# One half row of w2 loaded into 32 partitions by a transfer with an outer dimension of four

## The chip, the core and the metric

The kernel runs on one core of a Trainium2 chip. The metric is the time of one execution on the device in microseconds (us); the median of three runs of the kernel before is 138.66 us (138.64 to 138.8). Weights and caches lie in HBM (the chip's main memory). Transfers (DMAs) bring them to SBUF, the on-chip memory of 128 partitions; TensorE (PE) multiplies and writes its sums to PSUM; VectorE (DVE), ScalarE (ACT) and GpSimd (POOL) work on SBUF and PSUM; SyncE (SP) issues almost all of the transfers. A transfer is cut into packets, which are carried by 16 DMA engines; the profile's DMA row is the mean busy share of these 16.

## What is computed

One decoding step of a transformer block for four sequences (`x` is 4 x 1 x 1024), in bf16: attention over the last 2048 places of a key and value cache, then a gated feed-forward part.

```python
x = A_x
h = x + _A_ref(_layernorm(x), A_k_cache, A_v_cache, A_wq, A_wo)
# _B_ref(n) with n = _layernorm(h): B, D, F = 4, 1024, 3584
gate = einsum("bsd,df->bsf", n, w1)
up   = einsum("bsd,df->bsf", n, w3)
out  = einsum("bsf,fd->bsd", silu(gate) * up, w2)
h2 = h + out
```

With four sequences every weight is used once, so the kernel is above all a stream of 55.6 MB from HBM.

## The kernel before, in words

One function does everything. The order of the work on each engine is written out by hand (`manual_schedule`); the engines wait for each other by semaphores alone. All streamed data goes through one SBUF tile `ring` (128 partitions, five units of 16384 bf16 values each), whose regions are used again and again: a load must wait until the matmuls that read the old content are done. `load` (L123) issues on SP's queue, in the order wq (two pieces), four k blocks, four v blocks, wo, w1, w3, and then w2.

w2 has F = 3584 rows, viewed as `w2_v[p, fc, n]` with row p*28 + fc: each of the 128 partitions holds 28 of w2's rows, and "row fc" below is the slice of 128 x 1024 values with one fc. `W2B = [13, 8, 4, 2, 1]` (L114) cuts the 28 slices into five groups. The first 13 are loaded right behind w3; the others are issued after the gate matmuls (L507 to L512), the last slice in two halves of 512 columns. So w2 arrives in six transfers, each with its own semaphore, and each shorter than the one before it.

The feed-forward part runs so: gate matmuls (L494) on w1, silu on ACT and DVE (L513 to L516), up matmuls (also L494) on w3, the product `hg` and its transpose `hg_T` (L520, L521 with the helper's line L218). `hg_T[:, fc, :]` is the left operand for slice fc: 128 partitions x 32 columns. Then w2 is used in two styles:

- slices 0 to 20, the groups of 13 and 8: two matmuls of 512 columns each (L538), summed in the PSUM tile `early_ps`. DVE adds the result to `h1`, which holds the residual h (L549);
- slices 21 to 27, the groups of 4, 2 and 1: six matmuls each (L554), four of 128 columns and two of 256, summed in three PSUM tiles `y2_ps`. A matmul with a unit matrix (L565) adds part of `h1`, after the group of four.

At the end ACT copies and DVE adds into `res` (L577, L578, L582), and SP and ACT issue two small output transfers each (L587).

Early in the kernel `x` is loaded by ACT's queue (L135) into 16 partitions of `x_nat`, with a source view whose outer dimension is four, `x_flat.rearrange("b (c n) -> c b n", c=C)`, C = 4. POOL builds constants, a unit matrix `ident` among them (L144 to L183).

Of the kernel before, what the change touches and what calls it, by code (L numbers as in the profile page):

```python
# [10 lines left out]
P = 128  # L11
# [3 lines left out]
BF16 = mybir.dt.bfloat16  # L15
# [6 lines left out]
def kernel(  # L22
# [20 lines left out]
    nc = tc.nc  # L43

    B, _, D = A_x.shape
# [7 lines left out]
    FC = F // P  # L53
    NK = W // P
    C = 4
    R = 32
    S = R // B
    DQ = D // C
# [23 lines left out]
    w2_v = B_w2.rearrange("(p fc) n -> p fc n", fc=FC)  # L82

    const = ctx.enter_context(tc.tile_pool(name="const", bufs=1))
    act = ctx.enter_context(tc.tile_pool(name="act", bufs=1))
# [10 lines left out]
    ring = stream.tile([P, 5 * UNIT], BF16)  # L96

    def at(unit, *shape):
        o = unit * UNIT
        view = ring[:, o : o + int(np.prod(shape))]  # L100
        if len(shape) == 1:
            return view
        names = "abc"[: len(shape)]
        return view.rearrange(
            f"p ({' '.join(names)}) -> p {' '.join(names)}", **dict(zip(names, shape))
        )
# [4 lines left out]
    wo_s = at(3, T, D)  # L111
    w1_s = at(1, KC, F)
    w3_s = at(3, KC, F)
    W2B = [13, 8, 4, 2, 1]  # L114
    w2_s = []
    o = 0
    for i, n in enumerate(W2B):
        if i == 1:
            o = UNIT
        w2_s.append(ring[:, o : o + n * D].rearrange("p (a n) -> p a n", a=n))  # L120
        o += n * D

    def load(dst, src):  # L123
        nc.sync.dma_start(out=dst, in_=src)  # L124
# [13 lines left out]
    for b in range(B):  # L138
# [4 lines left out]
    ident = const.tile([P, P], BF16)  # L143
# [2 lines left out]
    nc.gpsimd.memset(mean_f[:], 1.0 / D)  # L146
    eps_t = const.tile([P, 1], FP32)
    nc.gpsimd.memset(eps_t[:], eps)
    ident_f = const.tile([P, P], FP32)
    nc.gpsimd.tensor_copy(out=ident_f[:], in_=ident[:])  # L150

# [6 lines left out]
        out=same[:], in_=t32[:].rearrange("p (o h) -> p o h", o=1).to_broadcast([P, C, R])  # L158
    )
    gmask = const.tile([P, 1, Hkv], BF16)  # L160
    with nc.allow_low_precision("sums of zeros and a single one"):
        nc.vector.tensor_reduce(
            out=gmask[:, 0], in_=t32[:].rearrange("p (g r) -> p g r", g=Hkv), axis=AX.X, op=ALU.add
# [3 lines left out]
    for j in range(JM):  # L167
# [3 lines left out]
        out=nscale[:], in_=ident_f[:2, :2], scalar=-qscale, op=ALU.mult  # L171
# [5 lines left out]
        out=place[:, : R * C].rearrange("p (h e) -> p h e", e=C)[:, :, C - 1], in_=t32[:]  # L177
# [6 lines left out]
        out=gather[:, :, :B], in_=ident[:].rearrange("p (c b s) -> p c b s", c=C, b=B)[:, :, :, 0]  # L184
# [31 lines left out]
    def transpose_quads(dst, src, n):  # L216

        nc.vector.transpose(  # L218
            out=dst.rearrange("p j r -> p (j r)"), in_=src.rearrange("p (q j) -> p j q", j=n)
        )  # L220
# [8 lines left out]
    for kc in range(KC):  # L229
        for hf in range(2):  # L230
            for c in range(C):
                o = (2 * c + hf) * HALF * Dh
                nc.tensor.matmul(  # L233
                    q_ps[R * c : R * c + R, hf],
                    lhsT=xn_T[:, kc, :],
                    rhs=wq_s[:, kc, o : o + HALF * Dh],
                    start=(kc == 0),
                    stop=(kc == KC - 1),
                    tile_position=(0, R * c),
# [5 lines left out]
    for r in range(REP):  # L245
# [8 lines left out]
        out=Qm[:].rearrange("p b (g y) -> p b g y", y=QW)[:, :, :, :REP],  # L254
        in_=qT_ps[:, :, :, :B].rearrange("p r g b -> p b g r"),
# [154 lines left out]
    small = ps.tile([P, 2, 512], FP32, tag="ktB")  # L410
# [29 lines left out]
    for e in range(C):  # L440
        nc.tensor.matmul(
            on_ps[:],
            lhsT=place[:, C - 1 - e : C - 1 - e + P],
            rhs=om[:, :, e * T : (e + 1) * T],
            start=(e == 0),
            stop=(e == C - 1),
# [6 lines left out]
    for i in range(2):  # L453
        for k in range(2):
            c = i + 2 * k
            nc.tensor.matmul(
                y_ps[R * i : R * i + R, k],
                lhsT=gather[:, c, :],
                rhs=x_nat[:],
                start=(k == 0),  # L460
                stop=False,
                tile_position=(0, R * i),
                skip_group_check=True,
            )
    for t in range(T):
        row = wo_s[:, t].rearrange("p (k i n) -> p i k n", k=2, i=2)
        for i in range(2):
            nc.tensor.matmul(  # L468
                y_ps[R * i : R * i + R],
                lhsT=oP[:, t, :],  # L470
                rhs=row[:, i],
                start=False,
                stop=(t == T - 1),
                tile_position=(0, R * i),
                skip_group_check=True,
            )
    load(w3_s, w3_v)
    load(w2_s[0], w2_v[:, : W2B[0], :])
    h1 = act.tile([P, DQ], FP32)
# [9 lines left out]
    def up_projection(w, out_ps):  # L489
        cols = w.rearrange("p k (c q h j) -> p k c h q j", c=C, h=2, j=FJ)  # L490
        for hf in range(2):
            for kc in range(KC):
                for c in range(C):
                    nc.tensor.matmul(  # L494
                        out_ps[hf][R * c : R * c + R, :],
                        lhsT=hn_T[:, kc, :],
                        rhs=cols[:, kc, c, hf],
                        start=(kc == 0),
                        stop=(kc == KC - 1),
                        tile_position=(0, R * c),  # L500
                    )
# [3 lines left out]
    eg = act.tile([P, 2, FH], FP32, tag="eg")  # L505
    hg = act.tile([P, 2, FH], BF16, tag="hg")
    up_projection(w1_s, [gate_ps[:, hf, :FH] for hf in range(2)])  # L507
    fc = W2B[0]
    for w, n in zip(w2_s[1:], W2B[1:]):
        for h in (slice(0, D),) if n > 1 else (slice(0, D // 2), slice(D // 2, D)):  # L510
            load(w[:, :, h], w2_v[:, fc : fc + n, h])
        fc += n  # L512
    nc.scalar.activation(out=eg[:], in_=gate_ps[:, :, :FH], func=ACT.Exp, scale=-1.0)  # L513
    nc.scalar.activation(out=eg[:], in_=eg[:], func=ACT.Identity, bias=1.0)  # L514
    nc.vector.reciprocal(out=eg[:], in_=eg[:])  # L515
# [2 lines left out]
    hg_T = act.tile([P, FC, R], BF16)  # L518
    for hf in range(2):
        nc.vector.tensor_tensor(out=hg[:, hf], in0=up_ps[hf][:], in1=eg[:, hf], op=ALU.mult)  # L520
        transpose_quads(hg_T[:, FJ * hf : FJ * hf + FJ, :], hg[:, hf], FJ)  # L521


    early_ps = ps.tile([2 * R, 2, DQ], FP32, tag="ktA", name="early_ps")
    DH = DQ // 2
    y2_ps = [
        ps.tile(shape, FP32, tag=tag, name="y2_ps")
        for shape, tag in (([P, DH], "scA"), ([P, DH], "ktB"), ([P, DQ], "scB"))
    ]
    NE = 2  # L530
    FE = sum(W2B[:NE])

    fc = 0
    for w, n in zip(w2_s[:NE], W2B[:NE]):
        for ff in range(n):
            row = w[:, ff].rearrange("p (k i n) -> p i k n", k=2, i=2)
            for i in range(2):
                nc.tensor.matmul(  # L538
                    early_ps[R * i : R * i + R],
                    lhsT=hg_T[:, fc, :],  # L540
                    rhs=row[:, i],
                    start=(fc == 0),
                    stop=(fc == FE - 1),
                    tile_position=(0, R * i),
                )
            fc += 1
    for k in range(2):
        part = h1[2 * R * k : 2 * R * k + 2 * R, :]
        nc.vector.tensor_tensor(out=part, in0=early_ps[:, k], in1=part, op=ALU.add)  # L549
    for m, (w, n) in enumerate(zip(w2_s[NE:], W2B[NE:])):  # L550
        for ff in range(n):
            for t, c, size in ((0, 0, DH), (0, 1, DH), (1, 0, DH), (1, 1, DH), (2, 2, DQ), (2, 3, DQ)):
                o = c * DQ + t % 2 * DH
                nc.tensor.matmul(  # L554
                    y2_ps[t][R * c : R * c + R, :],
                    lhsT=hg_T[:, fc, :],
                    rhs=w[:, ff, o : o + size],
                    start=(fc == FE),
                    stop=(fc == FC - 1),
                    tile_position=(0, R * c),  # L560
                    skip_group_check=True,
                )
            fc += 1
        if m == 0:
            nc.tensor.matmul(  # L565
                y2_ps[1][: 2 * R, :],
                lhsT=ident_f[:, : 2 * R],
                rhs=h1[:, DH:],
                start=False,
                stop=False,  # L570
                skip_group_check=True,
            )
    res = act.tile([P, DQ], BF16)
    for k in range(2):
        part = slice(2 * R * k, 2 * R * k + 2 * R)
        if k == 0:
            nc.scalar.copy(out=res[part, DH:], in_=y2_ps[1][part, :])  # L577
            nc.vector.tensor_tensor(  # L578
                out=res[part, :DH], in0=y2_ps[0][part, :], in1=h1[part, :DH], op=ALU.add
            )  # L580
        else:
            nc.vector.tensor_tensor(  # L582
                out=res[part, :], in0=y2_ps[2][part, :], in1=h1[part, :], op=ALU.add
            )
        for i, eng in enumerate((nc.sync, nc.scalar)):
            c = 2 * k + i
            eng.dma_start(  # L587
                out=out_flat[:, c * DQ : (c + 1) * DQ], in_=res[R * c : R * c + B, :]
# [31 lines left out]
```

## Time and profile before

| what | value |
|---|---|
| median of three runs | 138.66 us |
| the profiled execution: its own time | 138.7 us |
| its span, from first to last instruction | 136.7 us |
| PE, DVE, ACT, POOL busy share of the span | 55%, 37%, 21%, 11% |
| DMA queue of SP: share of 16 engines' span, bytes | 95.3%, 55.58 MB |
| mean rate from HBM over the span | 407 GB/s |
| granted TensorE clock, mean | 0.912 |

The span is 2.0 us shorter than the execution's own time: what lies before the first and behind the last instruction. The engines' shares say little here, since the DMA engines are busy nearly all the time. The page has further parts: the span in 40 slices, the DMA queues, the chain of waits that ended last, the costliest groups of instructions, and the DMA issues. Besides, a trace can be asked for a timeline, for the busy times in chosen stretches, and it keeps each DMA packet (its queue, size, start and duration) and each landing mark, the moment at which one DMA engine reports on a transfer's semaphore that its share is in place. The packets do not say which of the 16 engines carried them.

### The profile page before, as it was taken

How to read it: one execution, taken by the hardware profiler on the slowest of the kernel's cores; microseconds unless marked ns; L12 is line 12 of the kernel's file. 1: busy time of each engine (PE TensorE's matmuls, PEld its weight loads, DVE VectorE, ACT ScalarE, POOL GpSimd, SP SyncE). 2: the span in 40 equal slices, each digit the busy share in tenths (PEclk: the TensorE clock that was granted, in tenths of full speed). 3: DMA queues.
4: the chain of work that ended last, by engine and by line, in shares of the span. 5: the costliest groups of instructions: out<-in, count | busy, mean ns of one | idle time of the engine just before them, and what ended most of it. 6: DMA issues, size and time to landing. Idle time of an engine off the chain costs nothing.

```text
span 136.7 us, 1762 instructions
## 1 busy us (share of the span) xinstructions
PE 74.8 (55%) x762; PEld 40.6 (30%) x762; DVE 49.9 (37%) x50; ACT 28.8 (21%) x32; POOL 15.3 (11%) x41
## 2 busy tenths in 40 slices
PE   0000044959999986029966875994184000946471
PEld 0000011439957852014423323341042000413240
DVE  0000110006526363989799920004100594090022
ACT  3000130025968495104000000000405400000000
POOL 7300060000000000000176333000200000000000
PEclk9999999999999999955999999599959955599999
DMA  4999697999999999998978979969799798999960
GB/s 163 497 454 538 269 537 307 432 417 451 408 432 436 412 436 408 436 585 360 556 326 364 556 326 475 520 285 537 336 470 508 302 520 372 384 423 432 384 245 2
DMA packets 2795, 55.70 MB, mean 408 GB/s; under 512 B 324, under 2 KB 612, under 8 KB 740
## 3 DMA queue, kind: packets, MB, share of 16 engines
q1 hardware_dynamic: 2752, 55.58, 95.3%
q8 instruction: 6, 0.10, 0.3%
q10 hardware_dynamic: 36, 0.01, 0.0%
q14 instruction: 1, 0.01, 0.0%
HBM read 55.58 MB, written 0.01 MB: 407 GB/s over the span
## 4 chain that ended last, share of the span: by engine, by line
DMA 59%; PE 28%; DVE 6%; ACT 3%; SPq 1%; issue 1%; DVEq 0%
DMA ring<-in_B_w_dram 43%; DMA ring<-in_A_wq_dram 15%; PE kt_ps L267 9%; PE sc_ps L290 5%; PE q_ps L233 4%; PE o_ps L381 4%; PE gate L494 3%; DVE P L344 2%; DVE PT L366 2%; ACT ring L271 1%; PE small L381 1%; DVE ring L269 1%; SPq L124 1%; DVE rmax L302 1%; ACT q_sb L243 1%
## 5 line engine op out<-in xcount | busy, mean ns | idle before, releaser
L271 ACT COPY ring<-kt_ps 128x2048 bf16<-128x2048 bf16 x8 | 14.6, 1866 | 7.1 <-PE kt_ps L267 7.1
L267 PE MATMUL kt_ps<-ident,ring 128*128 128x128 bf16 x256 | 15.0, 219 | 0.6 <-DVE Qm L253 0.5
L267 PEld LDWEIGHTS <-ring 128*128 128x128 bf16 x256 | 14.4, 98 | 2.6 <-issue 2.6
L269 DVE COPY ring<-kt_ps 128x2048 bf16<-128x2048 bf16 x8 | 9.8, 1225 | 9.3 <-PE kt_ps L267 9.3
L398 POOL TENSOR_TENSOR o<-od 128x256 f32<-128x256 f32 x4 | 6.8, 1695 | 54.2 <-DVE od L389 54.2
L193 PE MATMUL sums_ps<-both,mean_f 128*128 128x64 f32 x4 | 1.1, 366 | 18.9 <-ACT both L191 18.9
L494 PE MATMUL up<-ring,n_T 128*32 128x448 bf16 x64 | 4.7, 467 | 12.2 <-DMA ring<-in_B_w_dram 12.2
L494 PEld LDWEIGHTS <-n_T 128*32 128x32 bf16 x128 | 4.2, 121 | 20.2 <-DMA ring<-in_B_w_dram 12.7
L344 DVE TENSOR_TENSOR P<-p,gmask 128x2048 bf16<-128x2048 bf16 x4 | 9.1, 2278 | 0.8 <-ACT p L331 0.8
L381 PEld LDWEIGHTS <-PT 128*128 128x128 bf16 x64 | 6.7, 107 | 9.0 <-issue 1.9
L366 DVE STREAM_TRANSPOSE PT<-P 128x2048 bf16<-128x2048 bf16 x4 | 9.2, 2306 | 0.1
L515 DVE RECIPROCAL eg<-eg 128x896 f32<-128x896 f32 x1 | 5.8, 5753 | 9.5 <-ACT eg L514 9.5
L468 PE MATMUL y_ps<-ring,oP 128*32 128x512 bf16 x64 | 8.8, 442 | 0.1
L233 PE MATMUL q_ps<-ring,n_T 128*32 128x512 bf16 x64 | 6.6, 587 | 3.8 <-DMA ring<-in_A_wq_dram 2.0
L381 PE MATMUL o_ps<-ring,PT 128*128 128x512 bf16 x32 | 8.6, 430 | 0.0
L290 PE MATMUL sc_ps<-ring,Qm 128*32 128x512 bf16 x64 | 7.6, 604 | 0.4 <-DVE ring L269 0.4
L538 PE MATMUL early_ps<-ring,hg_T 128*32 128x512 bf16 x42 | 4.9, 379 | 5.1 <-DMA ring<-in_B_w_dram 5.1
L381 PE MATMUL small<-ring,PT 128*128 128x512 bf16 x32 | 7.2, 379 | 0.7 <-DVE rinv L362 0.7
L193 PEld LDWEIGHTS sums_ps<-both,mean_f 128*128 128x128 f32 x4 | 0.8, 248 | 19.4 <-issue 16.9
L494 PE MATMUL gate<-ring,n_T 128*32 128x448 bf16 x64 | 4.6, 458 | 3.2 <-DMA ring<-in_B_w_dram 3.2
L577 ACT CAST res<-y_ps 64x128 bf16<-64x128 f32 x1 | 0.3, 259 | 26.3 <-PE y_ps L554 26.3
L218 DVE STREAM_TRANSPOSE x_T<-x_nat 128x256 bf16<-128x256 bf16 x1 | 0.6, 626 | 13.0 <-DMA x_nat<-in_A_x_dram 13.0
(81 smaller groups left out, 62.5 us busy)
## 6 DMA issues: line engine op xcount, KB each, us to landing
ring<-in_B_w_dram SPq DMA_DIRECT2D x2, 7168.0 KB
ring<-in_A_k_cache_dram SPq DMA_DIRECT2D x4, 2048.0 KB, 25.6
ring<-in_A_v_cache_dram SPq DMA_DIRECT2D x4, 2048.0 KB, 42.9
ring<-in_A_wq_dram SPq DMA_DIRECT2D x1, 7168.0 KB, 21.2
ring<-in_B_w_dram SPq DMA_DIRECT2D x1, 3328.0 KB
ring<-in_B_w_dram SPq DMA_DIRECT2D x1, 2048.0 KB
ring<-in_A_wq_dram SPq DMA_DIRECT2D x1, 1024.0 KB, 4.6
ring<-in_B_w_dram SPq DMA_DIRECT2D x1, 1024.0 KB, 28.1
```

Source lines behind the costliest of these rows:

```text
L233: nc.tensor.matmul(q_ps[R * c : R * c + R, hf], lhsT=xn_T[:, kc, :], rhs=wq_s[:, kc, o : o + HALF * Dh], start=(kc == 0), stop=(kc == KC - 1),
L267: nc.tensor.transpose(out=kt_ps[:, jj], in_=blocks[:, jj, :], identity=ident[:])
L269: nc.vector.tensor_copy(out=blocks, in_=kt_ps[:])
L271: nc.scalar.copy(out=blocks, in_=kt_ps[:])
L290: nc.tensor.matmul(sc_ps[b // 2][R * q : R * q + R, b % 2], lhsT=Qm[:, b, g * R : (g + 1) * R], rhs=kT[:, b, g, q], start=(g == 0), stop=( ...
L344: nc.vector.tensor_tensor(out=P4[:], in0=stage.pop(("p1", b))[:].rearrange("p (x o) -> p x o", o=1).to_broadcast([P, JR * L5, Hkv]), in1=g ...
L366: nc.vector.transpose(out=PT[:].rearrange("p j h -> p (j h)"), in_=stage.pop(("P4", b))[:].rearrange("p x g -> p (x g)"),)
L381: nc.tensor.matmul(o_ps, lhsT=PT[:, i * JM : (i + 1) * JM, :].rearrange("p j h -> p (j h)"), rhs=v_s[b][:, i * JM : (i + 1) * JM, :], star ...
L398: nc.gpsimd.tensor_tensor(out=o2[:], in0=od[:, :2], in1=od[:, 2:], op=ALU.add)
L468: nc.tensor.matmul(y_ps[R * i : R * i + R], lhsT=oP[:, t, :], rhs=row[:, i], start=False, stop=(t == T - 1), tile_position=(0, R * i), ski ...
L494: nc.tensor.matmul(out_ps[hf][R * c : R * c + R, :], lhsT=hn_T[:, kc, :], rhs=cols[:, kc, c, hf], start=(kc == 0), stop=(kc == KC - 1), ti ...
L515: nc.vector.reciprocal(out=eg[:], in_=eg[:])
```

## The change

The second half of w2's last slice is loaded as before. The first half, 128 rows of 512 values (1 KB each), goes into partitions 0 to 31 of `ring`, four rows in each: the view `w2_a` is 32 x 4 x 512. Its source is written with an outer dimension of four, an inner one of 32, and 512 values, and it is the first w2 transfer issued after the gate matmuls instead of the last but one. The groups become `[13, 8, 5, 1, 1]`. The rows then lie in another order in the partitions, so the left operands are brought into this order too: POOL builds `order`, four permuted pieces of the unit matrix; four small matmuls of `order` with the last slice of `hg_T` write `last_ps`, and ACT copies them to `last_T` (32 partitions x 4 x 32). The first half is then multiplied in four steps of 32 partitions, each step four matmuls of 128 columns (`FIRST`), right behind the early groups. The unit-matrix matmul stands before the group of five and reads 64 partitions of `h1` instead of 128. The two matmuls of 256 columns for the second half (`SECOND`) stand last.

```diff
-    W2B = [13, 8, 4, 2, 1]
+    W2B = [13, 8, 5, 1, 1]
...
+    T4 = P // R
+    w2_a = ring[:R, o : o + T4 * D // 2].rearrange("p (t n) -> p t n", t=T4)
...
+    order = const.tile([P, T4, C, R // C], BF16)
+    nc.gpsimd.tensor_copy(
+        out=order[:], in_=ident[:].rearrange("p (q t a) -> p t a q", t=T4, a=C)
+    )
...
     up_projection(w1_s, [gate_ps[:, hf, :FH] for hf in range(2)])
+    HALVES = (slice(0, D // 2), slice(D // 2, D))
+    load(w2_a, w2_v[:, FC - 1, HALVES[0]].rearrange("(y a) n -> a y n", a=C))
     fc = W2B[0]
-    for w, n in zip(w2_s[1:], W2B[1:]):
-        for h in (slice(0, D),) if n > 1 else (slice(0, D // 2), slice(D // 2, D)):
-            load(w[:, :, h], w2_v[:, fc : fc + n, h])
+    for w, n in zip(w2_s[1:-1], W2B[1:-1]):
+        load(w, w2_v[:, fc : fc + n, :])
         fc += n
+    load(w2_s[-1][:, 0, HALVES[1]], w2_v[:, FC - 1, HALVES[1]])
...
+    last_ps = small[:R, 1, : T4 * R].rearrange("p (t r) -> p t r", t=T4)
+    for t in range(T4):
+        nc.tensor.matmul(
+            last_ps[:, t],
+            lhsT=order[:, t].rearrange("p a q -> p (a q)"),
+            rhs=hg_T[:, FC - 1, :],
+            start=True,
+            stop=True,
+        )
+    last_T = act.tile([R, T4, R], BF16)
+    nc.scalar.copy(out=last_T[:], in_=last_ps)
...
+    early(0, 0)
+    early(1, W2B[0])
+    for t in range(T4):
+        late(w2_a[:, t], last_T[:, t], FIRST, start=(t == 0))
     for k in range(2):
         part = h1[2 * R * k : 2 * R * k + 2 * R, :]
         nc.vector.tensor_tensor(out=part, in0=early_ps[:, k], in1=part, op=ALU.add)
...
+    nc.tensor.matmul(
+        y2_ps[1][: 2 * R, :],
+        lhsT=ident_f[: 2 * R, : 2 * R],
+        rhs=h1[: 2 * R, DH:],
...
+    for fc in range(FE, FC - 1):
+        m, ff = (NE, fc - FE) if fc < FE + W2B[NE] else (NE + 1, 0)
+        row = w2_s[m][:, ff]
+        late(row, hg_T[:, fc, :], FIRST, stop=(fc == FC - 2))
+        late(row, hg_T[:, fc, :], SECOND, start=(fc == FE))
+    late(w2_s[-1][:, 0], hg_T[:, FC - 1, :], SECOND, stop=True)
```

`early` and `late` are the old loops as functions: `early` issues the 512-column matmuls of a group, `late` those that the tuple of cuts names.

More of the change, by code (lines that the diff above doesn't have):

```diff
@@ L531, with early, late @@
     FE = sum(W2B[:NE])
[L533 to L537, printed above, removed]
-                nc.tensor.matmul(
[L539 to L544, printed above, removed]
-                )
-            fc += 1
+    def early(i, fc):
+        for ff in range(W2B[i]):
+            row = w2_s[i][:, ff].rearrange("p (k i n) -> p i k n", k=2, i=2)
+            for i2 in range(2):
+                nc.tensor.matmul(
+                    early_ps[R * i2 : R * i2 + R],
+                    lhsT=hg_T[:, fc + ff, :],
+                    rhs=row[:, i2],
+                    start=(fc + ff == 0),
+                    stop=(fc + ff == FE - 1),
+                    tile_position=(0, R * i2),
+                )
+    FIRST = ((0, 0, 0), (0, 1, 0), (1, 0, DH), (1, 1, DH))
+    SECOND = ((2, 2, 0), (2, 3, 0))
+    def late(row, hT, cuts, start=False, stop=False):
+        for t, c, o in cuts:
+            out_ps = y2_ps[t][R * c : R * c + R, :]
+            nc.tensor.matmul(
+                out_ps,
+                lhsT=hT,
+                rhs=row[:, c * DQ + o : c * DQ + o + out_ps.shape[-1]],
+                start=start,
+                stop=stop,
+                tile_position=(0, R * c),
+                skip_group_check=True,
+            )
+    early(0, 0)
+    early(1, W2B[0])
+    for t in range(T4):
+        late(w2_a[:, t], last_T[:, t], FIRST, start=(t == 0))
     for k in range(2):
@@ L549 @@
         nc.vector.tensor_tensor(out=part, in0=early_ps[:, k], in1=part, op=ALU.add)
[L550 to L572, printed above, removed]
+    nc.tensor.matmul(
+        y2_ps[1][: 2 * R, :],
+        lhsT=ident_f[: 2 * R, : 2 * R],
+        rhs=h1[: 2 * R, DH:],
+        start=False,
+        stop=False,
+        skip_group_check=True,
+    )
+    for fc in range(FE, FC - 1):
[4 more added lines that the diff above has]
+    late(w2_s[-1][:, 0], hg_T[:, FC - 1, :], SECOND, stop=True)
     res = act.tile([P, DQ], BF16)
```

## The prediction

> **What bounds the kernel now.** I began with the chain of waits in order of time. Its last pieces (start, duration in us, what):
>
> ```profile
> 104.12 0.32 SPq L124
> 104.44 0.04 issue
> 104.48 0.43 SPq L124
> 104.91 0.04 issue
> 104.96 28.65 DMA ring<-in_B_w_dram
> 133.61 0.04 issue
> 133.65 0.30 PE y_ps L554 x2
> 133.95 0.02 issue
> 133.97 0.43 DVE res L582
> ```
>
> The last half of w2's last slice lands at 133.61; behind it stand two matmuls, one addition and the output, 3.1 us to the end of the span. So the end is set by the last landing. Is the queue full until then? The DMA view of 129 to 136.7 us says no (40 slices of 0.19 us, mean share of the 16 DMA engines in tenths), and busy time in chosen stretches says the same (the last three numbers are granted clock, DMA share, GB/s):
>
> ```profile
> DMA  9699999989995433426320000000000000000000
> ```
>
> ```profile
> 129.50:130.50 1.00, 1.00 (x14) 0.51 (x10) 0.00 (x0) 0.00 (x0) 0.00 (x0) 1.00 1.01 414
> 131.00:131.50 0.50, 0.06 (x2) 0.00 (x0) 0.41 (x1) 0.00 (x0) 0.00 (x0) 1.00 0.85 311
> 131.50:132.00 0.50, 0.33 (x18) 0.33 (x21) 0.43 (x2) 0.00 (x0) 0.00 (x0) 1.00 0.41 162
> 132.00:132.50 0.50, 0.50 (x19) 0.31 (x9) 0.00 (x0) 0.00 (x0) 0.00 (x0) 1.00 0.34 125
> ```
>
> From 131.5 on only some 0.34 to 0.41 of 16, about six engines, still carry data. The landing marks of the last transfer say it by engine: nine at 131.75 to 131.96, then 132.18, 132.94, 133.47, 133.48, 133.50, 133.60, 133.61. Five engines are 1.5 us late, one 0.8. Why shows in the list of queues:
>
> ```profile
> q1 hardware_dynamic: 2752, 55.58, 95.3%
> q8 instruction: 6, 0.10, 0.3%
> ```
>
> Six instruction fetches of 16 KB, each about 1.0 us on one engine, start at 34.07, 40.74, 50.54, 82.50, 105.63 and 132.56 in the packet records; after each of the first five one more engine's landing marks fall 1.3 us behind, for good. An 8 KB fetch of another queue at 119.12 delays the sixth. The total is set by the most loaded engine.
>
> **What the change does to the load of each engine.** It moves 128 KB from a transfer on all engines to one whose source has an outer dimension of four. The trace holds such transfers: the x load (source four pieces, 16 partitions) and the outputs. Their semaphores count 5 marks (one at once, four landings), all others 16; and the x load's 512-byte packets come four at a time (6.75, 6.79, 6.80, 6.82, then 8.89 and so on). So four engines carry it.
>
> [...] The trace agrees with the four (5 marks); that they are always the same four no run here shows. [...]
>
> Price of a packet: in the records a 1 KB packet takes 46 ns and the next starts 3 to 4 ns before its end, so 42.5 ns; for 4, 8 and 16 KB the step is 155, 306 and 607 ns, so 4.8 ns plus 37.7 ns per KB. Then:
>
> - on all engines: 8 packets of 1 KB and a mark fall away, -0.35 us (the late landings of the two old halves stand 0.34 to 0.36 apart);
> - on the four: 32 packets of 1 KB are added, 32 x 42.5 = 1.36 us, net +1.02;
> - groups 4 and 2 become 5 and 1: 8 x (306 + 155) against 8 x (382 + 80) ns, nothing.
>
> So every engine is 0.35 us earlier, but the four are 1.02 later. Bounds for the 24 KB more: 0.89 us at the 16 KB packets' rate, 1.3 at the longest 1 KB packet (54 ns); I take 1.02, from packets of the same size.
>
> **Are the late engines among the four?** That decides the sign. I take `w2_a` to use the same four as the x load; were it any other four of the 16, a free choice would miss all five late ones in 11 x 10 x 9 x 8 of 16 x 15 x 14 x 13 cases, 18%, which hardly changes the chances. On one engine each packet starts 3 to 4 ns before its predecessor's end, so the records can be linked into 16 strings. I followed the four strings that carry the x packets. The fetches at 34.07 and 82.50 surely hit others, that at 50.54 probably too, that at 40.74 is one of seven strings (two of them of the four). The string of the fetch at 105.63 goes back, without a break, to a tie of two strings at 45.5 us; one of these goes back to one of the four. Two signs favour that one: it needs one irregular gap at 24.2 us against two, and the lag from a string's last packet to its landing mark (about 30 ns higher on the one at 26 to 36 us, and on the one without the fetch from 51 us on). I call it 0.65 to 0.7 that this engine is one of the four, and a little over 0.7 that any fully late one is.
>
> The sum if so: this engine's last landing, the first of the five late, was 133.47; + 1.02 = 134.49, against 133.61: **+0.88 us**. What follows the landing is unchanged (two matmuls 0.30, addition 0.43, output). The profiled execution took 138.7, 0.04 above the median: 138.7 + 0.88 = 139.58, as a median **139.5**.
>
> **What costs nothing, and its cover.** `order`: one POOL copy, 0.2 to 0.29 us by the copies at L183 and L157; POOL is idle from 4.8 to 17.96 us, and its x_nat clearing, for which ACT's x load waits, stands ahead. The four `order` matmuls wait for hg_T (done 122.76) and stand ahead of the first early matmul, which starts at 124.35 when its data lands: 1.6 us of cover against at most 4 x 0.28 (the 256-column matmuls' mean); ACT's copy, some 0.26 (L577), has until 131. The 16 `FIRST` matmuls replace 4: by the last slices, 18 in 0.5 us, 16 take about 0.45; the early groups end near 131.05 and PE then waited 0.6 for data, so they fit; uncovered they would cost 0.45. In the forecast the group of eight lands 1.36 later on the slow engine (129.1 to 130.3) and the early matmuls end near 132.3; behind them wait the additions (0.87), the unit-matrix matmul (0.43) and the group of five, whose data lands only near 133.4: still covered. The loads: the first w2 issue now waits for a later gate matmul, 104.1 instead of 103.16, and four others stand behind it; SP's queue of data runs to 124.2 before they are needed, so 18 us of cover. Added PE instructions (32) bring the sixth fetch forward, from 132.56 to about the start of the group of five; on an engine already done it costs nothing, on one still loaded about 1.0 us.
>
> [...]
>
> **The rivals.**
>
> 1. *The four are free engines.* None of the fully late ones is hit: the four end at 131.96 + 1.02 = 132.98 at most, the late ones at 133.61 - 0.35 = 133.26, and the end comes 0.35 earlier: 138.66 - 0.35 = 138.3. For it: ten engines are idle 0.7 to 1.8 us, more than the 1.02 for most. Against it: the string of 105.63. It decides from one point on: no late engine among the four. Chance 0.22.
> 2. *Only the half-late engine* (fetch at 119.12, 132.94) is among the four: 132.94 + 1.02 = 133.96, +0.35, 139.0. One of four candidate strings is of the four, or two. Chance 0.08.
> 3. *It is spread over 16 engines after all*, so that the change does not do what it says: the load of each engine stays as it was and the last landing at 133.6, 138.7. Against it: the 5 marks of the x load. Chance 0.04.
>
> **How the numbers follow.** Forecast 0.66: 139.5, alone between 139.2 (0.89 for 1.02, and an engine that is 0.2 less late) and 139.9 (1.3 for 1.02). Rivals as above. With 0.66 + 0.08 + 0.04 two in ten would still be left out, so the range reaches down to rival 1: 138.25 to 139.95. A measurement here tells some 0.2%, 0.28 us, from no change. Rival 1 lies at -0.25%, so part of it counts as same: faster 0.18, same 0.09 (with rival 3), slower 0.73.
>
> **What would show it.** Right: the last transfer's landing marks reach from about 131.6 to 134.5, with at least one late alone; the DMA share in the last microsecond before the end is near one sixteenth to four sixteenths; the group of eight lands 1.2 us later than 129.11; PE waits for DMA last. Wrong: the last landing at 133.26 and marks closer together (rival 1); 16 marks for `w2_a` (rival 3); or a last wait that is PE's own, with data landed long before.

## The result, and the profile after

The changed kernel takes 140.62 us (median of four runs, 140.42 to 140.65), the kernel before 138.67 in the same job: a ratio of 1.0136, 95% interval 1.0118 to 1.0153, so +1.95 us. The profiled execution is the one of 140.42, with a span of 138.2, against 138.7 and 136.7 before.

The end of the chain of waits of the changed kernel (start, duration, what; SPq is SyncE issuing a load, the line DMA runs from the issue to the landing) has the form that it had before:

```profile
105.63 1.54 SPq L126
107.17 0.04 issue
107.22 0.44 SPq L126
107.69 27.42 DMA ring<-in_B_w_dram
135.12 0.04 issue
135.16 0.30 PE y_ps L571 x2
135.48 0.43 DVE res L611
```

The last landing still sets the end, with the same two matmuls and one addition behind it, but it comes at 135.12 instead of 133.61. The busy times in chosen stretches (start and end, length; PE, PEld, DVE, ACT, POOL busy with counts; then granted clock, DMA share, GB/s) show how few engines still carry data there:

```profile
132.50:133.00 0.50, 0.50 (x10) 0.11 (x6) 0.00 (x1) 0.00 (x0) 0.00 (x0) 1.00 0.58 219
133.00:133.50 0.50, 0.50 (x17) 0.37 (x13) 0.47 (x2) 0.00 (x0) 0.00 (x0) 1.00 0.39 135
133.50:134.00 0.50, 0.40 (x4) 0.25 (x3) 0.36 (x1) 0.00 (x0) 0.00 (x0) 1.00 0.06 23
134.00:134.50 0.50, 0.36 (x22) 0.36 (x25) 0.00 (x0) 0.00 (x0) 0.00 (x0) 1.00 0.07 25
```

From 133.5 on the share is 0.06 to 0.07, one engine of 16. The landing marks of the last transfer agree: seven at 132.25 to 132.82, eight at 133.64 to 134.03, and one alone at 135.12. The semaphore of `w2_a` counts five marks: one at once, then 124.22, 124.47, 125.06 and 126.33. So four engines carry it, and one of them is late.

So a late engine is among the four, as forecast; whether it is a fully late one, as forecast, or the half-late one, a_16p settles below. But the engines that carry nothing of `w2_a` come later than forecast too: the late ones of them were to end at 133.26, and the marks in front of the lone one reach 134.03. The same view of stretches dates the loss. First the changed kernel, then the kernel before:

```profile
122.00:123.00 1.00, 0.00 (x0) 0.00 (x0) 0.96 (x2) 0.00 (x0) 0.00 (x0) 1.00 1.14 435
123.00:124.00 1.00, 0.25 (x4) 0.14 (x3) 0.54 (x1) 0.11 (x1) 0.00 (x0) 1.00 1.17 296
124.00:125.00 1.00, 0.32 (x2) 0.13 (x4) 0.00 (x0) 0.14 (x1) 0.00 (x0) 0.74 0.82 243
125.00:126.00 1.00, 1.00 (x8) 0.36 (x6) 0.00 (x0) 0.00 (x0) 0.00 (x0) 0.50 0.99 361
```

```profile
122.00:123.00 1.00, 0.00 (x0) 0.00 (x0) 0.76 (x1) 0.00 (x0) 0.00 (x0) 1.00 0.99 422
123.00:124.00 1.00, 0.00 (x0) 0.00 (x0) 0.00 (x0) 0.00 (x0) 0.00 (x0) 1.00 1.00 426
124.00:125.00 1.00, 0.65 (x7) 0.37 (x9) 0.00 (x0) 0.00 (x0) 0.00 (x0) 1.00 0.96 410
125.00:126.00 1.00, 1.00 (x12) 0.57 (x10) 0.00 (x0) 0.00 (x0) 0.00 (x0) 1.00 0.92 393
```

The engines are as busy as before, yet they move less: 435 + 296 + 243 + 361 = 1335 KB in these four microseconds against 422 + 426 + 410 + 393 = 1651. The 316 KB missing are 0.76 us at some 415 GB/s. In the packet records, 32 of the 128 packets of 16 KB (the group of eight) take over 1.2 times their median of 0.62 us, the longest 1.18; before, the median was 0.614 and none took over 0.621. The slow ones start between 122.3 and 125.1, the time in which the four engines carry `w2_a`. This slowing is what the prediction lacked, and the experiments ask where it comes from.

### The profile page after: what moved, and what is told of

Same layout as the page of the kernel before. It is cut to its first block, busy times and chain, and to the rows that moved or that the text cites. A ratio compares the mean times of both kernels' runs of the same rounds, so it can differ in the third digit from the quotient of the medians.

```text
span 138.2 us, 1793 instructions
## 1 busy us (share of the span) xinstructions
PE 78.5 (57%) x776; PEld 42.1 (30%) x778; DVE 50.0 (36%) x50; ACT 29.0 (21%) x33; POOL 15.6 (11%) x42
## 4 chain that ended last, share of the span: by engine, by line
DMA 57%; PE 29%; DVE 6%; ACT 3%; SPq 2%; issue 1%; DVEq 0%
DMA ring<-in_B_w_dram 42%; DMA ring<-in_A_wq_dram 15%; PE kt_ps L273 9%; PE sc_ps L296 5%; PE o_ps L387 4%; PE gate L500 4%; PE q_ps L239 3%; SPq L126 2%; DVE P L350 2%; DVE PT L372 2%; ACT ring L277 1%; PE small L387 1%; DVE ring L275 1%; DVE rmax L308 1%; ACT q_sb L249 1%
## 5 line engine op out<-in xcount | busy, mean ns | idle before, releaser
L500 PE MATMUL up<-ring,n_T 128*32 128x448 bf16 x64 | 5.6, 533 | 11.4 <-DMA ring<-in_B_w_dram 11.4
L500 PEld LDWEIGHTS <-n_T 128*32 128x32 bf16 x128 | 4.8, 137 | 21.0 <-DMA ring<-in_B_w_dram 11.9
L387 PE MATMUL o_ps<-ring,PT 128*128 128x512 bf16 x31 | 11.0, 525 | 0.2 <-issue 0.2
L387 PEld LDWEIGHTS <-PT 128*128 128x128 bf16 x64 | 7.5, 119 | 10.1 <-issue 5.4
L556 PE MATMUL early_ps<-ring,hg_T 128*32 128x512 bf16 x42 | 6.5, 468 | 2.7 <-DMA ring<-in_B_w_dram 2.7
L239 PE MATMUL q_ps<-ring,n_T 128*32 128x512 bf16 x64 | 5.8, 525 | 3.6 <-DMA ring<-in_A_wq_dram 1.9
L500 PE MATMUL gate<-ring,n_T 128*32 128x448 bf16 x64 | 5.5, 528 | 3.6 <-DMA ring<-in_B_w_dram 3.6
L474 PE MATMUL y_ps<-ring,oP 128*32 128x512 bf16 x64 | 7.1, 379 | 0.1
```

The source lines that it names most:

```text
L239: nc.tensor.matmul(q_ps[R * c : R * c + R, hf], lhsT=xn_T[:, kc, :], rhs=wq_s[:, kc, o : o + HALF * Dh], start=(kc == 0), stop=(kc == KC - 1),
L387: nc.tensor.matmul(o_ps, lhsT=PT[:, i * JM : (i + 1) * JM, :].rearrange("p j h -> p (j h)"), rhs=v_s[b][:, i * JM : (i + 1) * JM, :], star ...
L474: nc.tensor.matmul(y_ps[R * i : R * i + R], lhsT=oP[:, t, :], rhs=row[:, i], start=False, stop=(t == T - 1), tile_position=(0, R * i), ski ...
L500: nc.tensor.matmul(out_ps[hf][R * c : R * c + R, :], lhsT=hn_T[:, kc, :], rhs=cols[:, kc, c, hf], start=(kc == 0), stop=(kc == KC - 1), ti ...
L556: nc.tensor.matmul(early_ps[R * i2 : R * i2 + R], lhsT=hg_T[:, fc + ff, :], rhs=row[:, i2], start=(fc + ff == 0), stop=(fc + ff == FE - 1) ...
```

## The experiments

"Own time" below is that of the profiled execution. The profiled execution of a_16p_at16 is the slowest of its runs; only its transfers are read here. "Slowed" counts, of the 128 packets of 16 KB in the group of eight, those over 1.2 times the median of the same 128 (0.614 to 0.624 us).

| run | median us | ratio (95%) | own time | last landing | slowed, longest us |
|---|---|---|---|---|---|
| before | 138.67 to 138.79 | | 138.7 | 133.61 | 0, 0.621 |
| after | 140.62 | 1.0136 (1.0118 to 1.0153) | 140.42 | 135.12 | 32, 1.178 |
| a_k16 | 139.87 | 1.0078 (1.0063 to 1.0093) | 139.6 | 134.30 | 29, 1.052 |
| b_4last | 139.48 | 1.0050 (1.0033 to 1.0067) | 139.5 | 134.34 | 0, 0.621 |
| b_4first | 140.19 | 1.0102 (1.0087 to 1.0117) | 140.35 | 135.04 | 40, 1.022 |
| a_pitch57 | 140.61 | 1.0130 (1.0113 to 1.0147) | 140.68 | 135.40 | 36, 1.200 |
| b_k16first | 138.85 | 1.0008 (0.9999 to 1.0017) | 138.79 | 133.54 | 0, 0.649 |
| a_16p | 139.99 | 1.0118 (1.0052 to 1.0184) | 139.59 | 134.28 | 0, 0.668 |
| a_16p_at16 | 141.47 | 1.0212 (1.0181 to 1.0244) | 142.9 | 136.34 | 32, 1.208 |
| a_16p_at32 | 139.99 | 1.0084 (1.0051 to 1.0117) | 139.42 | 134.14 | 0, 0.673 |
| b_more | 138.90 | 1.0014 (1.0005 to 1.0023) | 138.76 | 133.51 | 0, 0.621 |

One run of a_pitch57 took 143.01 and is not in its ratio. The four runs of a_16p lie far apart, at 139.32, 139.59, 140.38 and 141.35; the profile is that of 139.59.

### a_k16: the same target, an outer dimension of 32

```diff
-    load(w2_a, w2_v[:, FC - 1, HALVES[0]].rearrange("(y a) n -> a y n", a=C))
+    load(w2_a, w2_v[:, FC - 1, HALVES[0]].rearrange("(y a) n -> y a n", a=C))
...
-    order = const.tile([P, T4, C, R // C], BF16)
+    order = const.tile([P, T4, R], BF16)
```

`order` is built and read without the `a` dimension, since the rows now lie in their own sequence.

> The changed kernel with the 32-partition load spread over 16 DMA engines (source order 32 x 4 instead of 4 x 32, the unit matrix permuted to match); place in the queue, matmuls and copies stay. If the extra time comes from the concentration on four engines, in whichever way, it is gone: 138.5 to 138.9 us, and the 16 KB packets of the group of eight take 0.61 us again. If it comes from writing into partitions 0 to 31, from the place in the queue or from the added PE, POOL and ACT work, it stays near 140.6.

The source's outer dimension is 32 now, and the author took the load to be the same on every engine again; how many engines carry `w2_a` in this run is not shown. Yet the last landing is 134.30, against 133.61 in the kernel before, and 29 packets of the group of eight are slowed, the longest 1.052 us. So the slowing does not need the outer dimension of four, and, by that estimate, the four engines' extra load is not the whole loss.

### b_4last and b_4first: four engines, but 128 partitions

In the kernel before, only the first half's source view is changed; b_4first also issues it first:

```diff
# b_4last
-            load(w[:, :, h], w2_v[:, fc : fc + n, h])
+            if n == 1 and h.start == 0:
+                load(w[:, 0, h], w2_v[:, fc, h].rearrange("(y a) n -> a y n", a=C))
+            else:
+                load(w[:, :, h], w2_v[:, fc : fc + n, h])
# b_4first
+    first = slice(0, D // 2)
+    load(w2_s[-1][:, 0, first], w2_v[:, FC - 1, first].rearrange("(y a) n -> a y n", a=C))
...
+            if n > 1 or h.start:
+                load(w[:, :, h], w2_v[:, fc : fc + n, h])
```

> The kernel before with the first half of the last slice loaded through a source with outer dimension four, into all 128 partitions, in its old place (last but one); the rows stand in permuted order in the partitions and are used unpermuted, so half of the last slice's product is left wrong. Load theory (one late engine among the four, 24 KB more on it): last landing 133.61 to about 134.5, 139.5 to 139.6 us. Theory that the four-engine load also slows the others' packets: there are few others left at this place, so no more than 139.6 as well. If the four-engine load is slow by itself: over 140.

> As the run before, but with this load issued first of the loads behind the gate matmuls, ahead of the group of eight. Same bytes for each engine as there. Load theory alone: 139.5 to 139.6 as well. Slowing of the others' packets while the four engines carry it: about 0.9 us more, 140.3 to 140.7. If writing into 32 partitions is what slows, this run, which writes into 128, stays at 139.6.

That four engines carry it is taken from the five marks that the same source view had in the changed kernel. In the old place, with hardly any data left to carry, one mark lies alone at 134.34, +0.73 against 133.61, and the time is 0.7 longer. Part of that are its own packets: 59 of the 256 of 1 KB take over 1.2 times their median of 48 ns, up to 101. Issued first, with the group of eight behind it, the same transfer slows 40 packets and the last landing is 135.04, although it writes all 128 partitions. So the small target is not the cause either.

### a_pitch57: rows close together in HBM

From the changed kernel, with other rows as the source: those of one of its four pieces lie 57 KB apart instead of 229.

```diff
-    load(w2_a, w2_v[:, FC - 1, HALVES[0]].rearrange("(y a) n -> a y n", a=C))
+    load(w2_a, w2_v[:R, FC - C :, HALVES[0]].rearrange("y a n -> a y n"))
```

> The changed kernel with other source rows for the 32-partition load: the first 32 partitions' rows of slices 24 to 27, so that an engine's 32 rows stand 57 KB apart instead of 229 KB; still outer dimension four and 32 partitions; the product of the last slice's first half is left wrong. If the distance of the rows in HBM is what slows all packets from 122.5 to 125.3 us, these packets take 0.61 us and the time is 139.5 to 139.8; if it is the writing side or the four engines' small packets as such, 140.4 to 140.7.

36 slowed packets, the longest 1.200 us, and 140.61: nothing changes. Rows 57 KB apart are slowed as those 229 KB apart, so the distance is not the cause.

### b_k16first and a_16p: the size of the transfer, or whose partitions are written

```diff
# b_k16first, from the kernel before
+    first = slice(0, D // 2)
+    load(w2_s[-1][:, 0, first], w2_v[:, FC - 1, first])
...
+            if n > 1 or h.start:
+                load(w[:, :, h], w2_v[:, fc : fc + n, h])
# a_16p, from the changed kernel
+    w2_b = ring[:16, w2_at : w2_at + 8 * D // 2].rearrange("p (t n) -> p t n", t=8)
-    load(w2_a, w2_v[:, FC - 1, HALVES[0]].rearrange("(y a) n -> a y n", a=C))
+    load(w2_b, w2_v[:, FC - 1, HALVES[0]].rearrange("(y a) n -> a y n", a=C))
```

> The kernel before with the first half of the last slice (128 partitions, 16 engines, its old view) issued first of the loads behind the gate matmuls instead of last but one; nothing else. Theory 'size': 1 KB packets slow 16 KB packets that run beside them, wherever they are written: the group of eight shows packets of 0.7 to 1.0 us and the last landing comes some 0.7 later, 139.4 to 139.9 us. Theory 'place of writing': only packets that an engine writes into partitions other than the ones it writes in ordinary 128-partition loads slow the rest: 138.6 to 138.9 and no packet of the group over 0.65 us.

> The changed kernel with the four-engine load written into partitions 0 to 15, eight half rows in each, so that each of the four engines writes four neighbouring partitions instead of eight; source, packets and place in the queue stay, the matmuls read the old region, and the last slice's first half is left wrong. Theory 'place of writing' (each engine has its own groups of four partitions in ordinary loads): the slowing of the others is gone, 139.5 to 139.8. Theory 'size' (1 KB packets beside 16 KB ones): as the changed kernel, 140.4 to 140.7.

Many packets of 1 KB ahead of the group of eight do no harm by themselves (b_k16first: no packet over 0.649, +0.1 us), though they go to all 128 partitions. And with the four engines, the same 32 packets of 1 KB each and the same place, the slowing is gone as soon as they write 16 partitions instead of 32 (no packet over 0.668 us, against 1.178). The stretches of a_16p:

```profile
122.00:123.00 1.00, 0.00 (x0) 0.00 (x0) 0.97 (x2) 0.00 (x0) 0.00 (x0) 1.00 1.03 426
123.00:124.00 1.00, 0.25 (x4) 0.14 (x3) 0.53 (x1) 0.13 (x1) 0.00 (x0) 1.00 0.87 353
124.00:125.00 1.00, 0.79 (x6) 0.38 (x8) 0.00 (x0) 0.13 (x1) 0.00 (x0) 0.74 1.17 492
125.00:126.00 1.00, 1.00 (x8) 0.31 (x4) 0.00 (x0) 0.00 (x0) 0.00 (x0) 0.50 1.00 426
```

426 + 353 + 492 + 426 = 1697 KB, as much as before the change. The load shows pure: one mark alone at 134.28, the next at 133.18, where the prediction had 133.26 for the late engines that carry nothing of `w2_a`.

Without the slowing the string of packets on the lone engine can be followed back from its last 1 KB packet, which ends at 124.743: 32 packets, each starting 3 to 4 ns before the end of the one before, and what stands ahead of them (start in us, duration in ns, bytes; from the packet records of a_16p):

```
119.371   325   8192   instruction fetch
119.683  1649  26624
121.329   998  26624
122.323   991  26624
123.311     9      4   landing mark
123.316    46   1024   first of the 32
```

The late engine among the four is that of the 8 KB fetch at 119.37, the half-late one: the packet behind the fetch takes 1649 ns, those behind it 991 to 998. In a_16p_at32 and its two further profiles (the last section but one of this part) the same search ends at that string too (its 26 KB packets end at 123.168, 123.045 and 123.115, the first of six late engines each time; the other three of the four, by their landing marks of 123.86 to 124.06 in a_16p and a_16p_at32, began over 1 us earlier). The landing marks agree without any linking: from the first late mark of the group of 13 to the last mark of all it is 10.46 to 10.48 us in these four profiles; from the last of the late marks, that of a fully late engine, it is 9.79 to 10.11.

### a_16p_at16 and a_16p_at32: which sixteen partitions

In this layout each of the source's four pieces fills four neighbouring partitions; that each engine carries one piece is the author's estimate, from the 32 packets in the string above. Two kernels move it up by 16 and by 32:

```diff
-    w2_b = ring[:16, w2_at : w2_at + 8 * D // 2].rearrange("p (t n) -> p t n", t=8)
+    w2_b = ring[16:32, w2_at : w2_at + 8 * D // 2].rearrange("p (t n) -> p t n", t=8)
# or
+    w2_b = ring[32:48, w2_at : w2_at + 8 * D // 2].rearrange("p (t n) -> p t n", t=8)
```

> As a_16p, but written into partitions 16 to 31 instead of 0 to 15; the last slice's first half is left wrong. Theory 'own partitions': each engine writes certain groups of four partitions in ordinary loads, and here the four write groups of four other engines, so the group of eight has packets of 0.7 to 1.1 us again and the time is 140.0 to 140.7. Theory 'four partitions instead of eight for each engine': as a_16p, no packet over 0.67 us, last landing near 134.3, 139.4 to 139.7. [...]

> As a_16p, but written into partitions 32 to 47; the last slice's first half is left wrong. If an engine's own partitions are one run of eight neighbours (0 to 7 for the first), these belong to other engines and the slowing is back, 140.0 to 140.7. If they are two groups of four, 32 apart, the four write their own again: no packet of the group of eight over 0.67 us, 139.4 to 139.7. [...]

The stretches of a_16p_at16, then of a_16p_at32:

```profile
122.00:123.00 1.00, 0.00 (x0) 0.00 (x0) 0.97 (x1) 0.00 (x0) 0.00 (x0) 1.00 1.24 309
123.00:124.00 1.00, 0.25 (x4) 0.14 (x3) 0.01 (x1) 0.26 (x1) 0.00 (x0) 1.00 1.00 204
124.00:125.00 1.00, 0.00 (x0) 0.00 (x0) 0.00 (x0) 0.00 (x0) 0.00 (x0) 1.00 0.98 236
```

```profile
122.00:123.00 1.00, 0.00 (x0) 0.00 (x0) 0.96 (x2) 0.00 (x0) 0.00 (x0) 1.00 0.99 407
123.00:124.00 1.00, 0.25 (x4) 0.14 (x3) 0.44 (x1) 0.22 (x1) 0.00 (x0) 1.00 0.98 396
124.00:125.00 1.00, 0.73 (x4) 0.29 (x6) 0.00 (x0) 0.04 (x1) 0.00 (x0) 0.59 1.12 471
```

Sixteen partitions up, the rate falls to 204 GB/s, worse than after the change (243 at the lowest), and the last landing comes 2.2 us later (136.34 against 134.14). All engines are hit: the earliest mark of the last transfer comes at 132.86 against 131.32, the last but one at 134.70 against 133.24. Another sixteen up, nothing is slowed. So writing partitions 0 to 15 or 32 to 47 in this way slowed none of the 128 packets (the longest 0.668 and 0.673 us), writing 16 to 31 slowed 32 of them (up to 1.208). Partitions 16 to 31 are not slow in themselves: b_k16first sends packets of 1 KB there too, and nothing is slowed (the longest 0.649).

One reading fits the three runs, and it is the author's estimate: the engines that carry the half row in these runs write partitions 0 to 15 and 32 to 47 in the ordinary loads too, 16 to 31 belong to others, and the harm comes from writing where another engine writes. The packet records name neither their engine nor their partition, so no trace here shows which engine writes what, nor that the four are the same in each run.

### b_more: the side work alone

The kernel before with the POOL copy, 16 `order` matmuls (as many more PE instructions as the change adds, 32 with the weight loads) and ACT's copy; nothing of the loads is moved:

```diff
+    order = const.tile([P, T4, C, R // C], BF16)
+    nc.gpsimd.tensor_copy(
+        out=order[:], in_=ident[:].rearrange("p (q t a) -> p t a q", t=T4, a=C)
+    )
...
+    for u in range(4 * T4):
+        t = u % T4
+        nc.tensor.matmul(
...
+    nc.scalar.copy(out=last_T[:], in_=last_ps)
```

> The kernel before with the changed kernel's added side work and nothing moved: the POOL copy for order, 16 small matmuls of order with the last slice of hg_T (the four, four times over, so that PE has 32 instructions more, as the changed kernel), and ACT's copy to last_T, which nobody reads. If all of it is hidden: span 136.7, 138.6 to 138.8. All changed kernels so far showed 2.16 to 2.18 us between their span and their time, all versions of the old one 2.03: if the added instructions cause that, 138.8 to 138.95 with an unchanged span.

138.9: the span is 136.58, no longer than before (136.67), so the work is hidden. But 2.18 us lie outside the span, against 2.03 before. All versions of the changed kernel have 2.16 to 2.23, those of the kernel before without this work 2.03 or 2.04: +0.15 us that no instruction shows. Which part of the side work brings it was not separated.

### a_16p_look1 and a_16p_look2: two times of one kernel

a_16p_at32 had runs of 139.39 to 139.44 and of 140.54 to 140.63. a_16p_look1 and a_16p_look2 are the same kernel again, one profiled execution each.

> The kernel of a_16p_at32 again, for one look at its second time: its six runs were three near 139.4 and three near 140.55 us. If the second time comes from the last instruction fetch (131.1 in the trace at hand, on an engine that is not the most loaded) falling on the late engine of the four, a profile of it shows the fetch, the last landing near 135.3 alone, and no slow packets; a profile of the first time shows 134.1 to 134.3 as before. If it is PE's clock, the last landing stays near 134.2 and the time is lost behind it.

> As a_16p_look1, a second look, for the chance to see the other of the two times; the same expectations.

The first took 139.34, the second 140.37, with the last landing at 134.02 and 134.09. The two timelines of PE (start, duration, what, idle time before), a_16p_look1, then a_16p_look2:

```profile
124.28 4.67 PE L558 MATMUL early_ps<-ring,hg_T 128*32 128x512 bf16 x26 [0.44 <-DMA ring<-in_B_w_dram]
129.95 1.90 PE L558 MATMUL early_ps<-ring,hg_T 128*32 128x512 bf16 x16 [1.01 <-DMA ring<-in_B_w_dram]
...
133.05 1.30 PE L573 MATMUL y_ps<-ring,hg_T 128*32 128x128 bf16 x38 [0.25 <-DMA ring<-in_B_w_dram]
```

```profile
124.17 2.98 PE L558 MATMUL early_ps<-ring,hg_T 128*32 128x512 bf16 x26 [1.18 <-DMA ring<-in_B_w_dram]
130.02 3.37 PE L558 MATMUL early_ps<-ring,hg_T 128*32 128x512 bf16 x16 [2.86 <-DMA ring<-in_B_w_dram]
133.31 0.62 PE L573 MATMUL y_ps<-ring,last_T 32*32 32x128 bf16 x16
...
134.25 0.95 PE L573 MATMUL y_ps<-ring,hg_T 128*32 128x128 bf16 x38
```

In the first the 26 early matmuls of the group of 13 take 4.67 us instead of 2.98, in the second the 16 of the group of eight take 3.37 instead of 1.90. The stretches (in the same order) name the reason in the third number from the end, the granted clock:

```profile
126.00:127.00 1.00, 1.00 (x8) 0.33 (x6) 0.00 (x0) 0.00 (x0) 0.00 (x0) 0.50 0.94 397
...
131.00:132.00 1.00, 1.00 (x16) 0.44 (x14) 0.10 (x1) 0.00 (x0) 0.00 (x0) 1.00 0.62 235
```

```profile
126.00:127.00 1.00, 1.00 (x12) 0.41 (x9) 0.00 (x0) 0.00 (x0) 0.00 (x0) 1.00 0.92 391
...
131.00:132.00 1.00, 1.00 (x8) 0.35 (x4) 0.00 (x0) 0.00 (x0) 0.00 (x0) 0.50 0.61 237
```

The half clock falls once into a group that must wait for data behind it anyway (1.01 us idle), and once into the one behind which nothing waits: there PE is last, and the end of its work, at 135.20 instead of 134.35, sets the time. The rival, an instruction fetch on the late engine, falls, since that engine's last landing is the same.

### after_look2: the changed kernel once more

> The changed kernel once more, unaltered, to see what its slower executions (140.59 to 140.65, spans 138.4 to 138.5) hold beside the profiled one (140.42, span 138.2). If the landing decides in all of them, the last landing is within 0.1 us of 135.12 plus whatever the span is above 138.2, and the 16 early matmuls run at full clock (1.9 us). If TensorE's granted clock decides, as in the second look at the version with its own partitions, the last landing is at about 135.1, the 16 early matmuls behind the group of eight take about 3.4 us, and the chain of waits ends on PE. If it takes 140.4 again, this stays open.

It took 140.37, its own last landing is at 135.06 and one alone, 34 packets are slowed, and the 16 early matmuls take 1.90. So the profile of the change repeats, but the executions of 140.59 to 140.65 are in no profile; their 0.2 us stay open.

## Why the prediction was wrong

The direction was right: slower, by a late landing on an engine that is late already and one of four. The time, 140.62, lies 0.67 above the range. Two steps failed, with opposite signs.

**The step that failed by most** is in "What the change does to the load of each engine": "on all engines: 8 packets of 1 KB and a mark fall away, -0.35 us", and for the four, "net +1.02". It counted each engine's own packets at their price when all write undisturbed, and took the other engines to be independent of them. Between 122 and 126 us they are not: while the four write partitions 0 to 31, the packets of the group of eight take up to 1.18 us instead of 0.61. The row that would have priced this is not in the trace of before, since there every large load writes in the normal view; the bound of 1.3 for the 24 KB more, from the longest 1 KB packet, was a bound on the wrong quantity.

The sum, by the means of the profiles (after and after_look2; a_16p, a_16p_at32, a_16p_look1 and a_16p_look2):

| term | forecast | measured |
|---|---|---|
| load on a late engine: (134.28 + 134.14 + 134.02 + 134.09) / 4 = 134.13, less 133.61 | +0.88 | +0.52 (0.41 to 0.67) |
| slowing of all engines: (135.12 + 135.06) / 2 = 135.09, less 134.13 | 0 | +0.96 |
| from the landing to the end of the span: 3.12 less 3.06 | 0 | +0.06 |
| outside the span: 2.18 less 2.03 | 0 | +0.15 |
| sum, against 140.40 less 138.70 = 1.70 | +0.88 | +1.69 |

The medians are 1.95 apart; the 0.25 beyond the table lie in executions without a profile.

**"I call it 0.65 to 0.7 that this engine is one of the four"** is the other failed step. The engine of the fetch at 105.63 is not among them, nor is any fully late one: the strings of a_16p and its three relatives end at the 8 KB fetch. So the load goes as in rival 2, which had a chance of 0.08 and 132.94 + 1.02 = 133.96, +0.35. The error lies in the strings that were linked from 105 us back to the x packets at 7, through a tie and an irregular gap; the string that decides is some 5 us long, but it is found from a packet that only the changed kernel has.

**Four engines**: right. The forecast had them from the five marks of the x load; `w2_a` has five marks too, and the last transfer its lone landing. Rival 1 (four free engines) falls with that landing, rival 3 (16 engines) with the marks.

**The load term, "net +1.02" on the four,** stands nearly: 134.02 to 134.28 measured, 133.96 by rival 2. Of the 0.17 between that and the mean, 0.07 is that the 32 packets of a_16p take 1.43 us (123.316 to 124.743) and not 1.36; the rest lies within what the half-late engine varies by (its last mark is at 132.94 in the kernel before, 132.95 in b_k16first, 133.07 in b_more). The -0.35 us on all engines hold: the next marks are at 133.15 to 133.24 in these four profiles, forecast 133.26. The lower bound for the 24 KB more should have been 24 x 607 / 16 = 0.91 us, not 0.89, and eleven engines, not ten, were idle 0.7 us or more; neither matters here.

**"groups 4 and 2 become 5 and 1"**, at no cost, and the issue order on SP with 18 us of cover: right. The two groups take 2.50 + 1.30 = 3.80 us by the first landing marks before, and 3.10 + 0.68 = 3.78 in a_16p; and nothing in the chain behind 107.69 waits for an issue. SP's last issue took 5.86 us instead of 0.43, up to 113.55, and cost nothing, since the queue held data to carry for long after that (DMA share 0.92 from 113.6 to 119, 0.95 from 119 to 122).

**The sixth fetch** came at 132.15 in the changed kernel instead of 132.56; that the 32 added PE instructions moved it was the author's estimate, and by what a fetch is set off no run shows. It missed the engine that lands last: that engine's marks of the last four transfers stand 3.09, 0.67 and 0.35 us apart, those of the engine next to last 3.09, 0.69 and 0.33.

**The side work**, under "What costs nothing": right within the span, wrong by the 0.15 us outside it.

**"What follows the landing is unchanged"**: nearly, 3.12 us against 3.06.

**"Still covered"**, of the early matmuls: right in both profiles of the change (1.90 us, then 0.24 us of waiting for data), wrong where the half clock meets the group of eight, as a_16p_look2 shows. The reserve was worked out at full clock. There it is gone, and costs 140.37 - 139.34 = 1.03 us.

**What the sum would have given** without the slowing is seen in the kernels that write partitions 0 to 15 or 32 to 47: 139.34 to 139.59 in the three profiled executions where the landing decides, against a forecast of 139.5. That agreement is in part two errors that cancel: 0.36 less load, since another engine is the late one, and 0.21 more behind the landing.

No version here beats the kernel before: with the slowing gone, the four engines' extra load remains (last landing 134.02 to 134.28 against 133.61), and the half-late engine is one of them.

Open: which partitions each engine writes in the ordinary loads, why the last transfer lands later on all engines and not on some, why the profiled executions of the change are the quicker ones, and what made one run of a_16p 141.35. Whether the 8 KB fetch meets the same engine in every build of a kernel was not tried.

## What to carry to other kernels

A transfer has two prices: the packets of the engines that carry it, and what its target does to the others. Before a load is given another view, ask not only how many engines carry it, but also which partitions it writes: here 16 to 31 slowed the packets behind it (up to 1.21 us instead of 0.61), 0 to 15 and 32 to 47 did not. That each engine should write what it writes in the ordinary loads is the reading that fits, not a thing shown. If a load slows others, put it where nothing large follows it in the queue (b_4last: no packet slowed, +0.7 us; b_4first: 40 slowed, +1.4). And where a kernel ends on the last landing, sum the packets engine by engine, with the late ones by name: equal shares in bytes say little.

## What the runs showed of the hardware

- The load from a source with an outer dimension of four into partitions 16 to 31 slows the transfers of all 16 engines: packets of 16 KB take up to 1.21 us instead of 0.61, the rate falls to 204 GB/s where it was some 420 before the change, and the earliest mark of the last transfer comes at 132.86 instead of 131.32 (a_16p_at16 against a_16p_at32). Into partitions 0 to 15 and 32 to 47 it slows none (a_16p, a_16p_at32: no packet over 0.673).
- The slowing also comes with an outer dimension of 32 into 32 partitions (a_k16, 29 slowed packets) and with one of four into 32 (after, 32) and into 128 (b_4first, 40), and not with the ordinary view (b_k16first, none). All runs fit one reading, that the harm comes from writing partitions which another engine writes in the ordinary loads; it is an estimate, since no trace shows which engine writes which partition.
- Some work inside the kernel lengthens the time outside its span: 2.18 us instead of 2.03 (b_more).
- One kernel has two times, 139.4 and 140.5 (a_16p_at32). In the profiles of 139.34 and 140.37 (a_16p_look1, a_16p_look2) they differ by where the granted clock of 0.5 falls: on matmuls with a wait for data behind them, or without.
